# A delta rule with a low-rank mixer on one core: order estimated over all engines, two units' triangular blocks in 16x16, U^T x on four column groups

## Chip, core and metric

The kernel runs on one core of a Trainium2 chip. TensorE (PE; PEld is its loading of weights), VectorE (DVE), ScalarE (ACT), GpSimd (POOL) and SyncE (SP) each work through a queue of their own in order and wait for each other by semaphores. SP, ACT and POOL also issue transfers (SPq, ACTq, POOLq). The metric is device time in microseconds.

## What is computed

For 4 batches of 8 heads, 768 tokens and 48 channels: a delta rule with a state of 48x48 per head, and on its output, put together to 384 channels, a mixer with a matrix of rank 32 over tokens and two wide layers over channels. The inputs of the mixer (U, V, w_ch1, w_ch2) are float64; all else is float32.

```python
k_n = k / (norm(k) + 1e-6)
for t in range(768):
    y[t]  = q[t] @ state
    state = state + beta[t] * outer(k_n[t], v[t] - k_n[t] @ state)
x = y, heads side by side                 # (4, 768, 384)
u = x + ((x^T @ U) @ V)^T                 # rank 32 over tokens
out = u + relu(u @ w_ch1) @ w_ch2         # 384 -> 1536 -> 384
```

## The kernel before

**Units.** A batch is worked on in two units of 384 tokens (n = 0 to 7), a unit in six steps of 64 tokens, all heads together. `load` (line 256) fetches k, q, v of a unit by 24 transfers; `norms` (279) makes the norms of k and the factors cp; `grams` (325) transposes k and q on TensorE (p_t), copies them (kq) and multiplies k with k (pg) and k with q (qk). `blocks` (371) inverts a unitriangular 64x64 matrix per step and head: its two diagonal 32x32 blocks by substitution on VectorE, all 96 of a partition layout at once (gs is the blocks, fetched through HBM by scr; 31 steps of two instructions at lines 405 and 411, which write xt), then the block below by two rounds of 32x32 products on TensorE (p_x, p_v), for which xt goes through HBM (scr2) to zt and zc. `recur` (478) runs the steps: p_b (k times state), rhs, p_c (inverse times rhs), z, p_s (state's change), s, and two p_y.

**Mixer.** `front` (575) computes U^T x of a batch (p_tt, six matmuls into 32 partitions, then tt), adds V^T tt to x (p_h), and transposes x (p_u, ut); `wide` (616) runs the two wide layers on half a batch: p_f with relu (h_f), then p_o, a chunk being three matmuls (a float32 matmul is two instructions in the trace). `load_weights` (198) brings 27 slices of weights, whose float64 words VectorE and ScalarE turn into float32 by integer operations, five on VectorE a slice.

**Order.** Every part is a generator that yields what its next piece costs on TensorE and VectorE and a delay; `run` (96) takes, again and again, the piece that can start first by these numbers and lets it emit its instructions. What it emits first stands first in every engine's queue, SP's too; nothing is reordered later. PSUM has three pairs of buffers (pair, one, mix). In `load`, the next unit's loads start when the grams of the unit before are emitted and the recurrence two units back is done. Line 120 is the choice:

```python
start = max(ready[i], clock["pe"] if pe else 0, clock["dve"] if dve and not pe else 0)
```

Of the kernel before, what the change touches and what calls it, by code (L numbers as in the profile page):

```python
# [8 lines left out]
FP32 = mybir.dt.float32  # L9
# [6 lines left out]
L = 64  # L16
BK = 32
# [7 lines left out]
def kernel(  # L25
# [44 lines left out]
    step = ctx.enter_context(tc.tile_pool(name="step", bufs=3))  # L70
# [20 lines left out]
    done, clock = {}, {"now": 0.0, "pe": 0.0, "dve": 0.0}  # L91
# [4 lines left out]
    def run(parts):  # L96
        waits = {}
        ready = {}

        def advance(i, at):  # L100
            try:
                waits[i], ready[i] = next(parts[i]), at
            except StopIteration:
                waits.pop(i, None)

        for i in range(len(parts)):
            advance(i, 0.0)
        while waits:
            best = None
            for i in sorted(waits):  # L110
                step = waits[i]
                while i in waits and isinstance(waits[i][0], tuple):
                    keys = [k for k in waits[i] if k[1] >= 0]
                    if not all(k in done for k in keys):
                        break
                    advance(i, max([ready[i]] + [done[k] for k in keys]))
                if i not in waits or isinstance(waits[i][0], tuple):
# [3 lines left out]
                if best is None or start < best[0] - 1e-6:  # L121
                    best = start, i
            start, i = best
            pe, dve, after = waits[i]
            end = start + pe
            if pe:
                clock["pe"] = end
            if dve:
                end = clock["dve"] = max(end, clock["dve"]) + dve
            clock["now"] = end  # L130
            advance(i, end + after)
# [23 lines left out]

    bias_e = const.tile([128, 1], FP32, name="bias_e")
    nc.gpsimd.memset(bias_e, -896.0 * 2.0 ** 23)
    warm = const.tile([128, 1], FP32, name="warm")
    nc.scalar.sqrt(warm, ident[:, 0:1])
# [540 lines left out]
```

## Time and profile before

| what | us |
|---|---|
| median of 3 runs (lowest to highest) | 850.73 (849.42 to 859.04) |
| the profiled execution, whole | 850.8 |
| its span, first to last instruction | 849.1 |
| PE busy | 692.5 (82%) |
| PEld busy | 436.3 (51%) |
| DVE busy | 343.0 (40%) |
| ACT busy | 190.2 (22%) |
| POOL busy | 30.6 (4%) |
| mean granted TensorE clock, of full speed | 0.864 |

Busy shares are means over stages of different kinds. Matmuls are pipelined, so that the distance from the start of one to the start of the next says more than the duration of one. The chain that ended last is 55% PE, 17% DVE, 11% DMA and 8% SPq.

### The profile page before, as it was taken

What the parts mean: (1) busy time and instruction counts of PE and PEld (TensorE: products, weight loads), DVE (VectorE), ACT (ScalarE), POOL (GpSimd) and SP (SyncE); (2) the same over time, 40 slices, a digit from 0 to 9 for tenths busy, and PEclk for the clock granted to TensorE, in tenths of its full rate; (3) what the DMA queues carried; (4) which work ended last, traced back from release to release, by engine and by line L of the source; (5) the groups of instructions that cost most, each with busy time, mean ns of one, the idle gap of its engine ahead of it and who ended that gap; (6) DMA issues with size and microseconds to landing.
All of it is one profiled execution on the core that took longest, in us unless ns stands there. A gap on an engine that the chain in (4) does not pass through costs nothing.

```text
span 849.1 us, 17340 instructions
## 1 busy us (share of the span) xinstructions
PE 692.5 (82%) x7520; PEld 436.3 (51%) x7520; DVE 343.0 (40%) x884; ACT 190.2 (22%) x413; POOL 30.6 (4%) x59
## 2 busy tenths in 40 slices
PE   3430567758995899887989898998988999999998
PEld 2320565635553566563545565645555656455554
DVE  3659753474793831215728202166383101010000
ACT  2320213423320222232311133213320222021020
POOL 3100000020100000000000000000000000000000
PEclk9765555675997999986999999998989899999999
DMA  6722137172224020414040213041403000000000
GB/s 125 155 46 53 30 68 141 39 160 56 80 71 82 31 49 16 90 33 100 1 84 12 57 29 68 15 99 39 78 7 67 12 2 2 19 9 10 19 1 28
DMA packets 148083, 44.18 MB, mean 52 GB/s; under 512 B 141752, under 2 KB 144824, under 8 KB 148008
## 3 DMA queue, kind: packets, MB, share of 16 engines
q1 hardware_dynamic: 142720, 32.56, 19.2%
q0 software_dynamic: 2048, 9.83, 4.1%
q8 instruction: 59, 0.97, 0.5%
q10 hardware_dynamic: 3240, 0.69, 0.4%
q14 instruction: 16, 0.13, 0.1%
HBM read 31.95 MB, written 11.01 MB: 51 GB/s over the span
## 4 chain that ended last, share of the span: by engine, by line
PE 55%; DVE 17%; DMA 11%; SPq 8%; ACT 4%; issue 3%; POOL 1%; DVEq 0%; ACTq 0%; POOLq 0%
PE p_o L640 17%; PE p_f L623 17%; DVE xt L411 6%; DVE prod L405 5%; SPq L266 4%; PE p_c L524 3%; PE p_g L350 3%; DMA scr<-xt 3%; PE p_h L597 2%; PE p_y L554 2%; DMA gs<-scr 2%; PE p_t L338 2%; DMA scr<-pg 2%; PE p_s L538 2%; SPq L424 2%
## 5 line engine op out<-in xcount | busy, mean ns | idle before, releaser
L640 PE MATMUL p_o<-w_sb,h_f 128*128 128x384 f32 x576 | 209.2, 510 | 1.5 <-DVE w_sb L247 1.5
L623 PE MATMUL p_f<-ut,w_sb 128*128 128x384 f32 x576 | 208.1, 508 | 0.0
L640 PEld LDWEIGHTS p_o<-w_sb,h_f 128*128 128x128 f32 x576 | 108.1, 196 | 71.9 <-issue 11.9
L623 PEld LDWEIGHTS p_f<-ut,w_sb 128*128 128x128 f32 x576 | 108.0, 196 | 69.9 <-issue 8.7
L631 ACT ACTIVATE h_f<-p_f 128x384 f32<-128x384 f32 x96 | 47.1, 491 | 185.0 <-PE p_f L623 185.0
L411 DVE TENSOR_TENSOR xt<-xt,prod 96x31 f32<-96x31 f32 (+15 forms) x248 | 83.9, 338 | 8.7 <-DVE prod L405 0.3
L405 DVE TENSOR_TENSOR prod<-gs,xt 96x31 f32<-96x31 f32 (+15 forms) x248 | 83.4, 336 | 7.2
L647 DVE TENSOR_TENSOR x<-x,p_o 128x384 f32<-128x384 f32 x24 | 13.3, 553 | 131.8 <-PE p_o L640 131.8
L444 PE MATMUL p_x<-zt,pg 32*32 32x32 f32 x768 | 20.3, 216 | 49.9 <-DMA zt<-scr 49.7
L350 PE MATMUL p_g<-kq 48*64 48x128 f32 x768 | 36.1, 333 | 22.9 <-ACT kq L343 18.0
L547 DVE TENSOR_TENSOR s<-s,p_s 128x192 f32<-128x192 f32 x40 | 14.1, 352 | 91.8 <-PE p_s L538 91.5
L338 PE MATMUL p_t<-ident,qn 128*128 128x128 f32 x96 | 31.3, 341 | 23.9 <-DMA qn<-in_q_dram 18.8
L563 ACT COPY x<-p_y 64x192 f32<-64x192 f32 x96 | 30.1, 314 | 71.3 <-PE p_y L554 70.8
L444 PEld LDWEIGHTS p_x<-zt,pg 32*32 32x32 f32 x768 | 18.5, 131 | 53.4 <-issue 30.6
L350 PEld LDWEIGHTS p_g<-kq 48*64 48x64 f32 x768 | 27.1, 166 | 31.3 <-ACT kq L343 21.7
L508 DVE TENSOR_TENSOR rhs<-vn,p_b 128x192 f32<-128x192 f32 x44 | 15.4, 351 | 60.0 <-PE p_b L500 59.9
L524 PEld LDWEIGHTS p_c<-rhs,zt 64*64 64x64 f32 x704 | 29.0, 158 | 18.3 <-issue 11.3
L554 PE MATMUL p_y<-z,qk 64*64 64x48 f32 x768 | 37.0, 245 | 1.0 <-ACT z L532 1.0
L338 PE MATMUL p_t<-ident,kn 128*128 128x128 f32 x96 | 32.3, 352 | 6.2 <-DMA kn<-in_k_dram 4.2
L343 ACT COPY kq<-p_t 128x512 f32<-128x512 f32 x48 | 27.9, 584 | 37.0 <-PE p_t L338 34.7
L532 ACT COPY z<-p_c 128x192 f32<-128x192 f32 x48 | 15.3, 319 | 91.5 <-PE p_c L524 91.2
L524 PE MATMUL p_c<-rhs,zt 64*64 64x48 f32 x704 | 34.3, 245 | 1.8 <-DVE rhs L508 1.7
(71 smaller groups left out, 569.1 us busy)
## 6 DMA issues: line engine op xcount, KB each, us to landing
wide<-in_moe_w_ch_dram POOLq DMA_DIRECT2D x24, 384.0 KB, 3.7
vn<-in_v_dram SPq DMA_DIRECT2D x64, 72.0 KB
out_dram<-x SPq DMA_DIRECT2D x24, 192.0 KB
kn<-in_k_dram SPq DMA_DIRECT2D x60, 72.0 KB
qn<-in_q_dram SPq DMA_DIRECT2D x60, 72.0 KB
scr<-pg SPq DMA_DIRECT2D x32, 96.0 KB
gs<-scr SPq DMA_DIRECT2D x8, 384.0 KB
scr<-xt SPq DMA_DIRECT2D x8, 384.0 KB
```

The costliest lines, as they stand in the source:

```text
L266: queue.dma_start(out=t[L * g : L * g + L, :, s, 0:D], in_=src[b, 4 * g + s, hf * UC * L : (hf + 1) * UC * L, :].rearrange("(c t) d -> t c ...
L338: nc.tensor.transpose(p_t[:, j, i], t[:, c, 2 * j : 2 * j + 2].rearrange("p s d -> p (s d)"), ident,)
L350: nc.tensor.matmul(p_g[cols, par, c, :, j], kq[rows, c0 + c, j, 0, cols], kq[rows, c0 + c, j, :, cols], start=True, stop=True,)
L405: nc.vector.tensor_tensor(out=prod, in0=gs[:, j : j + 1, j + 1 :].to_broadcast([NP, m, w]), in1=xt[:, 0:m, j : j + 1].to_broadcast([NP, m, ...
L411: nc.vector.tensor_tensor(out=xt[:, 0:m, j + 1 :], in0=xt[:, 0:m, j + 1 :], in1=prod, op=ALU.subtract)
L444: nc.tensor.matmul(p_x[BK * g : BK * g + BK, r, BK * (e % (2 * UC)) : BK * (e % (2 * UC)) + BK], pg[rows, r, c, j, 0:BK], zt[rows, r, c, j ...
L524: nc.tensor.matmul(p_c[half(g), 2 * j + par], zt[half(g), par, cu, j], rhs[half(g), 2 * j + par], start=True, stop=True,)
L554: nc.tensor.matmul(p_y[half(g), par, D * j : D * j + D], qk[half(g), par, cu, j], z[half(g), 2 * j + par], start=(c == 0 and j == 0), stop ...
L563: nc.scalar.copy(x[half(c % 2), c // 2, 4 * D * g : 4 * D * (g + 1)].rearrange("p (j r d) -> p r j d", r=2, d=D), pair_of(p_y)[half(g)],)
L623: nc.tensor.matmul(p_f, w1_sb[:, t, f * 128 : (f + 1) * 128], ut[:, t], start=(t == 0), stop=(t == KT - 1),)
L631: nc.scalar.activation(h_f, p_f, ACTF.Relu)
L640: nc.tensor.matmul(p_o, hs[f][:, c * 128 - i * GT : (c + 1) * 128 - i * GT], w2_sb[:, f], start=(f == 0), stop=(f == FT - 1),)
```

## The change

It has three parts.

**The order.** A piece (`step`) now says what it costs on TensorE, VectorE, ScalarE and SP, which PSUM buffers it takes and which it gives back; `run` keeps a clock for each of the four and a list of free buffers. TensorE's costs count 1.6 times until the first `front`. Pieces are cut finer: a chunk's relu, a front's block of 128 tokens and an output row are parts of their own. Transposes go by k and q apart (two steps of k, or of q, in one p_t), and for units 0 and 1 the grams of k come ahead of those of q. Loads of k, q and v are pieces of four transfers each; q waits for the transposes of the unit before, k only for the recurrence two units back. The weights w_ch1 come by columns. beta and unit 0's v are issued on POOL. A slice of V is loaded four times, once for each 32 partitions.

**16x16.** For units 0 and 1 the substitution runs on the two 16x16 diagonal blocks of each 32x32 block (15 steps of two instructions, both blocks in one). Two rounds of products on TensorE, p_e and p_d, of 96 matmuls each with 32x32 weights and 16 columns, give the rest of the 32x32 block; p_d is written into zt by four ScalarE products and into zc by one VectorE instruction.

**U^T x.** Its six matmuls write four groups of 32 partitions (block c of tokens goes to group c % 4); V, standing four times, adds the groups up in p_h.

```diff
-                pe, dve, _ = waits[i]
-                start = max(ready[i], clock["pe"] if pe else 0, clock["dve"] if dve and not pe else 0)
+                engine = next((e for e in ("pe", "dve", "act", "sp") if s[e]), None)
+                at = max(
+                    [ready[i], clock[engine] if engine else 0.0]
+                    + [sorted(free[t])[s["take"].count(t) - 1] for t in s["take"]]
+                )
...
+            if s["pe"]:
+                ends["pe"] = clock["pe"] = at + s["pe"] * clock["slow"]
+            for e in ("dve", "act", "sp"):
+                if s[e]:
+                    ends[e] = clock[e] = max(clock[e], ends["pe"]) + s[e]
...
-        for t, src in ((kns[n % 2], k), (qn, q), (vn, v)):
+        for name, t, src in (("k", kns[n % 2], k), ("q", qn, q), ("v", vn, v)):
+            if name == "q":
+                yield need(("turned", n - 1))
             for g in range(2):
+                queue = nc.sync
+                if n == 0:
+                    queue = nc.gpsimd if name == "v" else (nc.sync, nc.scalar)[g]
+                yield step(sp=2.6 if queue is nc.sync else 0.0)
...
+        split = 2 if n < 2 else 1
+        SB = BK // split
...
-        for j in range(BK - 1):
-            m, w = j + 1, BK - 1 - j
+        for j in range(SB - 1):
+            m, w = j + 1, SB - 1 - j
...
+                for i in range(4):
+                    rows = slice(BK * i, BK * i + BK)
+                    nc.tensor.matmul(
+                        p_e[rows, e],
+                        pg[rows, r, c, j, BK * (i % 2) : BK * (i % 2) + BK],
+                        zc[rows, e, SB:BK],
...
+                    nc.tensor.matmul(
+                        p_d[rows, e], zn[rows, e], xe[rows, e], start=True, stop=True
+                    )
...
+                nc.scalar.mul(diagonal(zt, i)[0:SB, :, SB:BK], p_d[rows], -1.0)
...
-            p_t = ps_one([R, DM], "p_tt")
+            p_t = ps_one([128, DM], "p_tt")
             for c in range(NB):
...
-                    p_t, u_sb[:, c], x[:, c], start=(c == 0), stop=(c == NB - 1)
+                    p_t[R * (c % 4) : R * (c % 4) + R], u_sb[:, c], x[:, c],
+                    start=(c < 4), stop=(c + 4 >= NB),
```

Three places show how instructions moved. The first is SP's queue from the program's start; kn0 and kn1 are the keys of units 0 and 1, xt and pg of unit 0 come first. Before:

```order
L266 DMA kn0_92<-in_k_dram 64x6x48 x4
L266 DMA qn_94<-in_q_dram 64x6x48 x4
L266 DMA vn_117<-in_v_dram 64x6x48 x8
L316 DMA cp_247<-cts_245 24x32 x4
L266 DMA kn1_93<-in_k_dram 64x6x48 x8
L266 DMA qn_94<-in_q_dram 64x6x48 x8
L266 DMA vn_337<-in_v_dram 64x6x48 x8
L381 DMA scr_365<-pg_143 32x24x32 x4
L388 DMA gs_370<-scr_365 96x1024
```

And of the change:

```order
L309 DMA kn0_92<-in_k_dram 64x6x48 x4
L309 DMA qn_94<-in_q_dram 64x6x48 x4
L309 DMA kn1_93<-in_k_dram 64x6x48 x8
L360 DMA cp_291<-cts_264 24x32 x4
L455 DMA scr_365<-pg_120 32x24x32 x4
L360 DMA cp_408<-cts_381 24x32 x4
L464 DMA gs_450<-scr_365 96x1024
L455 DMA scr_545<-pg_125 32x24x32 x4
L309 DMA qn_94<-in_q_dram 64x6x48 x4
L464 DMA gs_577<-scr_545 96x1024
L309 DMA qn_94<-in_q_dram 64x6x48 x4
L509 DMA scr2_599<-xt_493 96x1024
```

Unit 1's q and v moved behind unit 0's scr and gs, its cp ahead of gs, and unit 0's v left the queue. The second place is TensorE's queue in the third and fourth step of the first recurrence, where the change has put unit 1's p_e (before, no other work stood there until p_x):

```order
L659 MATMUL p_b<-s,kq 64x48 x8
L667 MATMUL p_y<-s,kq 64x48 x8
L553 MATMUL p_e<-zc,pg 32x16 x24
L684 MATMUL p_c<-rhs,zt_95 64x48 x8
L553 MATMUL p_e<-zc,pg 32x16 x24
L699 MATMUL p_s<-z,kn_92 64x48 x8
L707 MATMUL p_y<-z,qk 64x48 x8
L553 MATMUL p_e<-zc,pg 32x16 x24
```

Each piece of 24 matmuls stands where TensorE's next step waits for rhs, z or s. The third place is TensorE's queue around the first U^T x. Before, with kn_93 and qn being unit 3's keys and queries:

```order
L554 MATMUL p_y<-z,qk 64x48 x8
L585 MATMUL p_tt<-x,u_sb 32x384 x6
L338 MATMUL p_t<-ident,kn_93 128x128
L338 MATMUL p_t<-ident,qn 128x128
L338 MATMUL p_t<-ident,kn_93 128x128
L338 MATMUL p_t<-ident,qn 128x128
L597 MATMUL p_h<-tt,v_sb 128x384
```

And of the change:

```order
L754 MATMUL p_tt<-x,u_sb 32x384 x6
L768 MATMUL p_h<-tt,v_sb 128x384 x2
L776 MATMUL p_u<-ident,x 128x128 x6
L768 MATMUL p_h<-tt,v_sb 128x384
L776 MATMUL p_u<-ident,x 128x128 x3
L768 MATMUL p_h<-tt,v_sb 128x384 x2
L809 MATMUL p_f<-ut,w_sb 128x384 x3
L776 MATMUL p_u<-ident,x 128x128 x6
L809 MATMUL p_f<-ut,w_sb 128x384 x3
L768 MATMUL p_h<-tt,v_sb 128x384
L385 MATMUL p_t<-ident,kn_93 128x128 x4
```

Unit 3's transposes moved behind the front and two chunks of p_f.

## Rows read from the trace of the kernel before

**Rows 1.** Timeline of TensorE (start us, us, engine, line, operation): the four U^T x.

```profile
178.19 5.91 PE L585 MATMUL p_tt<-x,u_sb 128*32 128x384 f32 x12
...
381.70 6.55 PE L585 MATMUL p_tt<-x,u_sb 128*32 128x384 f32 x12
...
562.32 4.06 PE L585 MATMUL p_tt<-x,u_sb 128*32 128x384 f32 x12
...
731.46 4.06 PE L585 MATMUL p_tt<-x,u_sb 128*32 128x384 f32 x12
```

**Rows 2.** Page, part 2: clock granted to TensorE, 40 slices, tenths of full speed.

```profile
PEclk9765555675997999986999999998989899999999
```

**Rows 3.** Timeline: ScalarE's last copy of unit 0's pg, and SP's queue.

```profile
25.53 5.40 SPq L266 DMA_DIRECT2D kn<-in_k_dram  x8
...
30.90 0.59 ACT L358 COPY pg<-p_g 128x512 f32<-128x512 f32 x1 [0.79 <-PE p_g L350]
...
41.83 2.40 SPq L381 DMA_DIRECT2D scr<-pg  x4
```

**Rows 4.** Timeline: unit 0's substitution on VectorE: first, a middle and last instruction.

```profile
49.61 1.22 DVE L392 TENSOR_TENSOR gs<-gs,cp 96x1024 f32<-96x1024 f32 x1 [10.54 <-DMA gs<-scr]
...
69.08 0.42 DVE L405 TENSOR_TENSOR prod<-gs,xt 96x256 f32<-96x256 f32 x1
...
80.86 0.21 DVE L411 TENSOR_TENSOR xt<-xt,prod 96x31 f32<-96x31 f32 x1
```

**Rows 5.** Timeline: unit 0's p_x and the first p_c.

```profile
89.86 2.77 PE L444 MATMUL p_x<-zt,pg 32*32 32x32 f32 x94 [1.66 <-DMA zt<-scr]
...
97.18 0.45 PE L524 MATMUL p_c<-vn,zt 64*64 64x48 f32 x2 [0.90 <-ACT zt L465]
```

**Rows 6.** Timeline of TensorE: the product that turns beta.

```profile
5.79 2.74 PE L175 MATMUL p_bt<-ident,beta_sb 16*64 16x16 f32 x46 [1.04 <-DMA beta_sb<-in_beta_dram]
```

**Rows 7.** Timeline of TensorE: p_b of two recurrence steps that follow each other.

```profile
105.95 0.68 PE L500 MATMUL p_b<-s,kq 48*64 48x48 f32 x16 [0.74 <-ACT x L563]
...
110.87 0.68 PE L500 MATMUL p_b<-s,kq 48*64 48x48 f32 x16 [0.74 <-ACT x L563]
```

**Rows 8.** Page, part 6 (KB each, us to landing), and VectorE's groups until 260 us.

```profile
wide<-in_moe_w_ch_dram POOLq DMA_DIRECT2D x24, 384.0 KB, 3.7
...
L243 DVE SCALAR_TENSOR_TENSOR power<-wide,power 128x384 int32<-128x384 int32 (+2 forms) x27 | 14.6, 542 | 5.8 <-ACT power L230 5.8
```

**Rows 9.** Timeline of TensorE: p_x between other work.

```profile
312.80 1.70 PE L444 MATMUL p_x<-zt,pg 32*32 32x32 f32 x94 [0.44 <-DMA zt<-scr]
314.43 0.67 PE L524 MATMUL p_c<-rhs,zt 64*64 64x48 f32 x16
```

**Rows 10.** Timeline of TensorE: a step of the second batch's recurrence, with chunks.

```profile
294.31 0.45 PE L500 MATMUL p_b<-s,kq 48*64 48x48 f32 x16 [1.06 <-DVE s L551]
...
294.92 2.20 PE L623 MATMUL p_f<-ut,w_sb 128*128 128x384 f32 x6
...
297.05 0.67 PE L524 MATMUL p_c<-rhs,zt 64*64 64x48 f32 x16
...
302.75 0.45 PE L500 MATMUL p_b<-s,kq 48*64 48x48 f32 x16
```

**Rows 11.** Timeline and chain: a p_h, and 12 chunks behind each other.

```profile
737.58 0.91 PE L597 MATMUL p_h<-tt,v_sb 32*128 32x384 f32 x2
...
822.10 23.23 PE p_o L640 x72
```

**Rows 12.** Timeline of TensorE: four transposes, the chunk behind them, and one gram.

```profile
418.82 0.27 PE L338 MATMUL p_t<-ident,kn 128*128 128x128 f32 x1
...
419.26 1.13 PE L623 MATMUL p_f<-ut,w_sb 128*128 128x384 f32 x3
...
423.67 1.10 PE L350 MATMUL p_g<-kq 48*64 48x128 f32 x32
```

**Rows 13.** Timeline of TensorE behind the first U^T x.

```profile
193.03 0.48 PE L338 MATMUL p_t<-ident,qn 128*128 128x128 f32 x1 [6.84 <-DMA qn<-in_q_dram]
```

More of the change, by code (lines that the diff above doesn't have):

```diff
@@ L88, in ps_mix, with need, step, advance @@
         return psum.tile(shape, FP32, name=name, tag="mix", bufs=2)
-    done, clock = {}, {"now": 0.0, "pe": 0.0, "dve": 0.0}
+    done = {}
+    clock = dict(now=0.0, pe=0.0, dve=0.0, act=0.0, sp=0.0, slow=1.6)
+    free = dict(pair=[0.0] * 2, one=[0.0] * 2, mix=[0.0] * 2)
+    def need(*keys):
+        return [k for k in keys if k[1] >= 0]
+    def step(pe=0.0, dve=0.0, act=0.0, sp=0.0, then=0.0, on=None, take=(), give=()):
+        return dict(pe=pe, dve=dve, act=act, sp=sp, then=then, on=on, take=take, give=give)
     def emitted(key, after=0.0):
         done[key] = clock["now"] + after
[L96 to L107, printed above, removed]
+    parts, waits, ready = {}, {}, {}
+    def advance(i, at):
+        try:
+            waits[i], ready[i] = next(parts[i]), at
+        except StopIteration:
+            del waits[i]
+    def begin(part, place):
+        i = (place, len(parts))
+        parts[i], waits[i] = part, []
+        advance(i, clock["now"])
+    def run():
         while waits:
@@ L120, in run @@
-                start = max(ready[i], clock["pe"] if pe else 0, clock["dve"] if dve and not pe else 0)
[L121 to L131, printed above, removed]
+                while isinstance(waits.get(i), list) and all(k in done for k in waits[i]):
+                    advance(i, max([ready[i]] + [done[k] for k in waits[i]]))
@@ new lines, in run @@
+                if best is None or at < best[0] - 1e-6:
+                    best = at, i
+            at, i = best
+            s = waits[i]
+            for t in s["take"]:
+                free[t].remove(min(free[t]))
+            ends = {"pe": at}
+            if s["pe"]:
[3 more added lines that the diff above has]
+                    ends[e] = clock[e] = max(clock[e], ends["pe"]) + s[e]
+            clock["now"] = max(ends.values())
@@ L134 @@
+            for t in s["give"]:
+                free[t].append(clock["now"] + 0.1)
+            advance(i, ends.get(s["on"], clock["now"]) + s["then"])
     ident = const.tile([128, 128], FP32, name="ident")
@@ L181, in beta_thread @@
                 )
+        yield step(dve=0.4, give=("one",))
         nc.vector.tensor_copy(out=betas, in_=p_bt)
@@ L250, in load_weights @@
             )
[L251 removed]
+            emitted(("weights", i), 0.2)
     raw, made, xs, states = {}, {}, {}, {}
@@ L308, in norms @@
         )
-        yield 0.3, 1.3, 0.5
+        yield step(pe=0.2, then=0.15, take=("one",))
         p_ct = ps_one([CS, 128], "p_ct")
@@ L440, in blocks @@
+        yield step(dve=1.0, then=-0.8)
+        zn = turned(zc)
+        place = [slice(64 * split // 2 * g, 64 * split // 2 * g + BK) for g in range(2)]
         for e in range(CS):
+            if e % 8 == 0:
+                yield step(pe=0.57, take=("pair",) if e == 0 else ())
+            if e == 0:
+                p_x = ps_pair("p_x")
             r, c, j = e // (2 * UC), e // 2 % UC, e % 2
@@ L519, in recur @@
                     )
-            yield 0.6, 0, 0.9
+                yield step(dve=0.37, then=0.1, give=("pair",))
+                rhs = steps.tile([128, 4, D], FP32, name="rhs", bufs=2)
+                nc.vector.tensor_tensor(
+                    out=by_slot(rhs), in0=by_slot(vn), in1=pair_of(p_b), op=ALU.subtract
+                )
+            yield step(pe=0.4, then=0.1, take=("one",))
             p_c = ps_one([128, 4, D], "p_c")
```

435 lines of the change are left out of this document (270 added, 165 removed).

## The prediction, on record before the changed kernel was run

> **What bounds the kernel now.** I read the page's 40 slices first, then the order of time of TensorE, SP and VectorE. The four places where U^T x of a batch starts on TensorE [rows 1] cut the span of 849.1 us into five pieces: 178.2 until the first, then 203.5, 180.6 and 169.2 from one to the next, and 117.6 from the last to the end. In the first piece nothing of the wide layers can run, since the first batch's recurrence must end first; the clock granted to TensorE there is half, 1.2 of 2.4 GHz, for most of it [rows 2]. It is a chain of small steps: loads, grams, scr and gs through HBM, VectorE's substitution, the joining of the 32x32 blocks, twelve recurrence steps. In the three middle pieces one batch's wide layers (48 chunks of three matmuls) run between the next batch's recurrence steps: TensorE's work is the bound there as long as its queue is not stuck at a wait. The last piece is the last batch's wide layers alone.
>
> **The sum's form.** New time = A (to the first U^T x) + 3 C (one batch to the next) + D (last U^T x to the end) + 1.7, the part of the profiled execution's 850.8 that lies outside its span. The median shown, 850.73, is the same, so the result stands against it too.
>
> **A, the first piece (178.2 now).** Unit 0's pg is complete at 31.5, but SP issues unit 1's 24 loads first, from 25.53 on, so that scr<-pg stands at 41.83, and VectorE, waiting for gs, begins at 49.61 [rows 3, 4]. In the new SP order scr comes ahead of unit 1's q and v. Two things hold it: the four cp transfers of unit 1, now between scr and gs (about 3.2), and ScalarE, whose four q issues stand behind the first weight conversion; I take pg at 32.5, scr issued by 35, cp to 38.6, gs landed and VectorE free at 42.5: 7 earlier.
>
> The substitution of unit 0 takes until scr2 at 81.1 now, 31.5, with unit 1's norms in it. New: 15 steps of two instructions on two small blocks of 30 to 128 elements. A row of 31 elements takes 0.21, one of 256 takes 0.42 [rows 4]; on that line the mean is 0.27, 0.30 from start to start: 9.0, with half a gs product and one qk 10. End: 52.5. What was moved with it: scr2, then four v loads of unit 1 (2.8 of SP), then four zc; I take zc landed at 61, 8.5 behind, as p_x now begins 8.8 behind the substitution [rows 4, 5].
>
> Added: the join. p_e and p_d are 192 instructions each of 32x32 weights and 16 columns. The nearest row is p_x, 94 in 2.77 at half clock, 29.5 ns each [rows 5]; the other end is p_bt, 16 columns with other weights, 46 in 2.74, 60 ns [rows 6]. I take p_x, whose weights have the same shape: 5.7 each; the other end adds 5.8 to each. With unit 1's transposes and grams between the pieces of p_e (2.6), its copy (0.7) and the four ScalarE products from p_d (2.0), the first half of the join is over at 78. From p_x to p_c takes 7.3 now [rows 5]; a second xz copy and ScalarE's conversions in front make it 9.4: the recurrence starts at 87.4 instead of 97.2. So unit 0 gains only 9.8, although its substitution is 21 shorter.
>
> The recurrence: a step at half clock takes 4.92 [rows 7], twelve take 59; today the stretch takes 81, since unit 1's zt, unit 2's loads and grams are waited for in order. New: 59, plus p_e and p_d of unit 1 in eight pieces between the steps (11.4, of which I let 9 count, since TensorE waits little in a step), p_x and p_v 5.5, unit 2's transposes and grams 8, and 3 for the weights: two slices a step now stand ahead of rhs and s on VectorE. A slice lands in 3.7 and takes VectorE five instructions of about half a microsecond (one is the 0.542 of the row) [rows 8]; with two buffers that is one per about 3.1, 6.2 a step for six steps, partly beside p_e. That is 84.5: **A = 172**, 6 less than now.
>
> Weighed here: p_x (32x32 weights) and the p_c behind it (64x64) start 1.63 apart, which is what 94 instructions of 17 ns take; no gap for the change of shape is to be seen [rows 9]. The Trainium skill ("TensorEngine Tiling (Array Packing)", Tiling Modes, Key Properties) says that a change of tiling mode drains TensorE, which speaks against pieces of p_e and p_d between 64x64 work. Were each of the sixteen changes to cost 0.4, the sum would be 6 higher; by the row it is nothing.
>
> **C, batch to batch (203.5, 180.6, 169.2 now).** TensorE's work in one: a recurrence step with three chunks takes 8.44, a chunk in it 2.13, so the step itself 2.05 [rows 10]; a chunk behind another chunk takes 23.23 / 12 = 1.94 [rows 11]. In the new order 43 of 48 chunks stand alone: 101.3. Steps 24.6; twelve groups of four transposes at 0.44 and six grams at 1.1: 11.9 [rows 12]; p_x and p_v four times 1.63: 6.5 [rows 9]; six p_h at 0.9, 5.4 [rows 11]; p_u 2.0; U^T x. U^T x takes 4.0 now [rows 1]. On four column groups: nothing before shows this form. The ends are 4.0, if the groups run one after the other, and 1.2: grams in four tiles pass 128 columns in 1.1/32 = 0.034 a piece where whole-array transposes take 0.11 [rows 12], 3.2 times as many. I take 1.7. The sum is 153.4; with today's U^T x 155.7.
>
> Today's order leaves three chunks behind the third U^T x and five behind the fourth. With that made even the three pieces are 203.5, 187 and 173.4, so 48, 31 and 18 are lost to waits and to the half clock behind them. Part of it is unit 3's transposes, queued directly behind U^T x with loads that SP has not yet issued: TensorE stands 6.84 at one of them [rows 13]. In the new order p_h, p_u and the first p_f come first; by the prices above unit 3's k is needed 16 behind U^T x and has landed 10 behind, p_x of unit 2 is reached 53 behind and its zt has landed 49 behind, p_x of unit 3 at 95 against 91. Also, all weight conversions are over by then; today they lie between unit 2's substitution steps. What is left to lose: the end of the recurrence and the front are uncovered now (U^T x waits for the last x, tt, x and ut one for another, 4 to 5), and behind such waits part of the front runs at half clock (4), and 2 elsewhere: 10.6. **C = 164.**
>
> **D (117.6 now).** Without the five chunks left over, 107. U^T x saves 2.3, the front loses its cover, 8 as above: **D = 113**.
>
> Sum: 172 + 492 + 113 + 1.7 = **779**.
>
> **Rivals.**
> First, the clock: the denser first piece lifts TensorE's clock before the first U^T x. For it: pieces of p_e and p_d fill waits; against: today's busy recurrence stays at half [rows 2]. The steps would fall from 4.92 to what VectorE's weights allow, and A to about 154: 761. Chance 0.15.
> Second, the join is dearer than p_x: at p_bt's 60 ns [rows 6] it adds 11 on unit 0's chain and about 8 between the steps, A = 191: 798. The zc path through HBM, shared with v loads, would show in the same place. Chance 0.20.
> Third, the estimated order does not keep TensorE fed: each C loses the 18 of today's best piece, C = 171.4: 801. For it: the queues are in order and the estimates are numbers; against: the distances of 4 and more found above. Chance 0.13.
> Fourth, U^T x does not run side by side; that part of the change then does nothing: 2.3 in each of four, 788. Chance alone 0.04.
> Fifth, not faster at all: the weights. All 27 slices now stand on VectorE ahead of the first batch's last steps; if the other loads, moved beside them, delay the slices, each late slice stops rhs and s. 71 over 24 slices are 3.0 each; with two buffers a slice must then land in 9.7 instead of 3.7 for the time to reach 850. For it: all loads of units 0 and 1 share the first 60 us; against: the median of 3.7 holds today beside the same loads [rows 8]. Chance 0.04.
> The forecast itself: 0.44.
>
> **How the numbers follow.** 779 is the likeliest case. Below it lies the first rival at 761, above it the others at 788 to 801; A's own error is some 10 and C's 3 for each of three, so I give 752 to 813, which leaves out the fifth rival and the tails of the first and third. A change within 1% is about what a measurement of this kernel can't tell from none: only cases between the fifth rival and the others would land there, 0.02; slower by over 1%, 0.04; faster, 0.94.
>
> **What would show it.** U^T x starting near 172, 336, 500 and 664; gs on VectorE near 42.5; substitution of unit 0 over near 52.5; p_c of unit 0 near 87; p_e and p_d near 5.7 each for 192; U^T x under 2 when its x is there; between two U^T x no wait over 2 at p_x or at transposes. I am wrong if A stays at 178 or more, if C stays above 172, or if VectorE waits for weight slices during the recurrence.

## Result, and the profile after

The changed kernel takes 731.71 us (median of 4 runs, 726.95 to 737.04) against 851.93 of the kernel before beside it: a ratio of 0.858, 95% interval 0.850 to 0.866. The forecast was 779 with a range of 752 to 813: right in its sign, wrong in its size. The profiled execution took 726.95, with a span of 725.1, and is the fastest of the four.

The rows that answer to [rows 1] and [rows 2] are the four U^T x, in TensorE's timeline (start us, us, engine, line, operation), and the page's clock row:

```profile
162.04 1.83 PE L754 MATMUL p_tt<-x,u_sb 128*32 128x384 f32 x12
...
314.64 1.83 PE L754 MATMUL p_tt<-x,u_sb 128*32 128x384 f32 x12
...
467.33 1.83 PE L754 MATMUL p_tt<-x,u_sb 128*32 128x384 f32 x12
...
616.61 2.59 PE L754 MATMUL p_tt<-x,u_sb 128*32 128x384 f32 x12
```

```profile
PEclk9975555599999999999999999999999999999999
```

The view by windows shows the five pieces that these starts cut: first of the changed kernel, then of the kernel before (busy us of each engine with its instructions, then TensorE's granted clock, DMA share, GB/s).

```profile
core 0: us, PE busy (x) PEld busy (x) DVE busy (x) ACT busy (x) POOL busy (x), PEclk, DMA share, GB/s
0.00:162.04 162.04, 99.31 (x2667) 85.37 (x2667) 102.27 (x260) 59.36 (x118) 33.51 (x70) 0.68 0.57 125
162.04:314.64 152.60, 150.52 (x1873) 94.10 (x1869) 70.54 (x187) 43.59 (x97) 3.64 (x4) 1.00 0.27 56
314.64:467.33 152.69, 150.51 (x1873) 94.10 (x1869) 70.63 (x187) 43.58 (x97) 3.60 (x4) 1.00 0.27 56
467.33:616.61 149.28, 145.66 (x1752) 89.62 (x1748) 65.24 (x177) 37.15 (x85) 1.21 (x2) 1.00 0.22 45
616.61:725.10 108.49, 102.66 (x332) 59.24 (x330) 7.21 (x13) 14.97 (x32) 0.00 (x0) 0.99 0.03 11
```

```profile
178.19:381.70 203.51, 172.15 (x1870) 106.12 (x1868) 99.44 (x252) 50.38 (x109) 10.29 (x17) 0.89 0.28 64
381.70:562.32 180.62, 162.50 (x1853) 98.48 (x1851) 71.73 (x191) 43.94 (x98) 2.37 (x4) 0.92 0.23 49
562.32:731.46 169.14, 156.70 (x1743) 94.09 (x1742) 62.72 (x170) 37.10 (x84) 1.18 (x2) 0.94 0.16 34
731.46:849.10 117.64, 113.05 (x355) 63.59 (x354) 8.30 (x15) 14.33 (x30) 0.00 (x0) 0.99 0.04 14
```

Of the 107.8 that the last four pieces lost (670.9 to 563.1), 52.8 are idle time of TensorE (66.5 to 13.7 over the four) and 55.0 are busy time. U^T x itself is 12.5 of the busy time (20.6 to 8.1 over the four); the rest goes along with the granted clock, at which nearly the same instructions pass: its mean in the four pieces was 0.89, 0.92, 0.94 and 0.99 and is 1.00, 1.00, 1.00 and 0.99. In a middle piece TensorE is now busy for 150.5 of 152.6.

The first piece, by the timeline (for [rows 4] and [rows 5]): VectorE's first and last instruction of unit 0's substitution, a piece of 48 of p_e, most of p_d, the first p_c.

```profile
40.90 0.68 DVE L478 TENSOR_TENSOR gs<-gs,cp 96x512 f32<-96x512 f32 x1
...
50.57 0.21 DVE L501 TENSOR_TENSOR xt<-xt,prod 96x30 f32<-96x30 f32 x1
```

```profile
64.20 0.84 PE L553 MATMUL p_e<-zc,pg 32*32 32x16 f32 x48
...
67.88 1.90 PE L570 MATMUL p_d<-xe,zn 32*32 32x16 f32 x128 [0.97 <-issue]
...
84.74 0.44 PE L684 MATMUL p_c<-vn,zt 64*64 64x48 f32 x2 [1.97 <-ACT zt L623]
```

### The profile page after: what moved, and what is told of

Read it like the earlier page. It is cut to its first block, busy times and chain, and to the rows that moved or that the text cites. A ratio compares the mean times of both kernels' runs of the same rounds, so it can differ in the third digit from the quotient of the medians.

```text
span 725.1 us, 19244 instructions
## 1 busy us (share of the span) xinstructions
PE 648.7 (89%) x8480; PEld 422.4 (58%) x8480; DVE 315.9 (44%) x824; ACT 198.6 (27%) x426; POOL 42.0 (6%) x80
## 4 chain that ended last, share of the span: by engine, by line
PE 80%; DMA 6%; DVE 3%; issue 3%; SPq 3%; ACT 2%; POOL 2%; ACTq 0%; DVEq 0%; POOLq 0%
PE p_o L825 27%; PE p_f L809 26%; PE p_c L684 4%; PE p_y L707 3%; PE p_g L400 3%; PE p_t L385 3%; PE p_s L699 2%; DMA wide<-in_moe_w_ch_dram 2%; PE p_b L659 2%; SPq L309 2%; PE p_v L616 2%; PE p_x L595 2%; DMA gs<-scr 2%; PE p_y L667 2%; PE p_h L768 1%
## 5 line engine op out<-in xcount | busy, mean ns | idle before, releaser
L809 PE MATMUL p_f<-ut,w_sb 128*128 128x384 f32 x576 | 203.4, 494 | 0.6 <-ACT ut L779 0.6
L825 PE MATMUL p_o<-w_sb,h_f 128*128 128x384 f32 x576 | 201.2, 495 | 0.0
L809 PEld LDWEIGHTS p_f<-ut,w_sb 128*128 128x128 f32 x576 | 103.6, 190 | 61.5 <-issue 1.5
L501 DVE TENSOR_TENSOR xt<-xt,prod 96x112 f32<-96x112 f32 (+21 forms) x216 | 70.5, 326 | 7.7 <-DVE prod L495 0.3
L495 DVE TENSOR_TENSOR prod<-gs,xt 96x112 f32<-96x112 f32 (+21 forms) x216 | 70.1, 324 | 6.5
L400 PE MATMUL p_g<-kq 48*64 48x128 f32 (+1 forms) x960 | 32.5, 285 | 11.1 <-ACT kq L391 11.1
L707 PEld LDWEIGHTS p_y<-z,qk 64*64 64x64 f32 x768 | 30.5, 152 | 0.6 <-ACT z L693 0.6
L699 PEld LDWEIGHTS p_s<-z,kn 64*64 64x64 f32 x704 | 16.1, 149 | 25.2 <-issue 16.1
L385 PE MATMUL p_t<-ident,qn 128*128 128x128 f32 x96 | 18.1, 317 | 12.6 <-DMA qn<-in_q_dram 12.6
L419 DVE TENSOR_TENSOR qk<-p_g,mask_u 128x256 f32<-128x256 f32 x48 | 18.0, 416 | 23.8 <-ACT pg L413 23.8
```

Source lines behind the costliest of these rows:

```text
L385: nc.tensor.transpose(p_t[:, x, j], t[:, c, 2 * j : 2 * j + 2].rearrange("p s d -> p (s d)"), ident,)
L400: nc.tensor.matmul(p_g[cols, par, c, parts, j], kq[rows, c0 + c, j, 0, cols], kq[rows, c0 + c, j, parts, cols], start=True, stop=True,)
L495: nc.vector.tensor_tensor(out=prod, in0=gb[:, :, j : j + 1, j + 1 :].to_broadcast([NP, split, m, w]), in1=xb[:, :, 0:m, j : j + 1].to_broa ...
L501: nc.vector.tensor_tensor(out=xb[:, :, 0:m, j + 1 :], in0=xb[:, :, 0:m, j + 1 :], in1=prod, op=ALU.subtract,)
L699: nc.tensor.matmul(p_s[half(par), g, D * j : D * j + D], kn[half(g), cu, 2 * j + par], z[half(g), 2 * j + par], start=True, stop=True,)
L707: nc.tensor.matmul(p_y[half(g), par, D * j : D * j + D], qk[half(g), par, cu, j], z[half(g), 2 * j + par], start=(c == 0 and j == 0), stop ...
```

## Experiments

All runs in one table: time (ratio to the kernel before beside it, with interval), and the five pieces of the profiled execution.

| kernel | us | ratio (95%) | to first U^T x | 2nd | 3rd | 4th | last |
|---|---|---|---|---|---|---|---|
| before | 850.73 | | 178.2 | 203.5 | 180.6 | 169.1 | 117.6 |
| changed | 731.7 | 0.858 (0.850-0.866) | 162.0 | 152.6 | 152.7 | 149.3 | 108.5 |
| e_one_group | 760.6 | 0.892 (0.886-0.898) | 165.9 | 159.2 | 157.8 | 155.5 | 114.5 |
| e_whole32 | 750.2 | 0.881 (0.876-0.886) | 160.6 | 176.7 | 156.3 | 148.9 | 107.3 |
| e_order_only | 784.1 | 0.920 (0.911-0.928) | 160.3 | 180.9 | 168.8 | 156.4 | 114.3 |
| e_old_order | 846.8 | 0.993 (0.989-0.997) | 190.0 | 191.6 | 179.8 | 168.7 | 109.0 |
| e_one_group_wide_h | 739.5 | 0.866 (0.860-0.872) | 169.6 | 154.2 | 154.1 | 151.2 | 111.7 |
| e_narrow_h | 750.5 | 0.879 (0.875-0.884) | 170.1 | 157.6 | 156.9 | 152.9 | 110.9 |
| e_keep_clock | 737.7 | 0.865 (0.861-0.870) | 173.3 | 151.8 | 153.6 | 148.7 | 107.5 |
| e_join_by_tile | 745.5 | one run | 181.7 | 152.5 | 153.1 | 148.7 | 107.5 |
| e_four_tiles | 728.2 | 0.845 (0.839-0.852) | 172.1 | 150.0 | 150.6 | 148.0 | 107.3 |
| e_late_tt | 764.6 | 0.892 (0.885-0.899) | 170.2 | 160.9 | 160.6 | 156.5 | 116.4 |
| e_full_speed | 732.6 | 0.855 (0.848-0.861) | 156.2 | 165.1 | 151.8 | 149.1 | 107.5 |
| e_no_act_clock | 729.0 | 0.850 (0.844-0.857) | 156.2 | 160.0 | 153.6 | 149.9 | 107.6 |
| b_long_trip | 844.8 | 0.987 (0.979-0.994) | 171.3 | 204.4 | 179.7 | 172.2 | 117.6 |
| e_short_trip | 769.4 | 0.899 (0.893-0.904) | 171.8 | 166.8 | 161.5 | 161.6 | 107.4 |
| b_wide_h | 840.9 | 0.982 (0.974-0.990) | 183.0 | 200.4 | 180.0 | 162.4 | 115.6 |

The first piece differs between executions of the same program part: the changed kernel, e_one_group and e_narrow_h have the same order up to the first U^T x, which stands at 162.0, 165.9 and 170.1. Their first p_c is at 84.7 to 86.2; what differs with it is when the granted clock rises from 0.5 to 1.0: at 147.8, at 156.3, and in e_narrow_h only at 172.1, behind the first U^T x. Why it rises earlier in one execution than in another is not shown. So runs are compared here by the pieces behind it; one profiled execution stands for each run.

### The parts apart

e_one_group (U^T x on one group, p_h on 32 rows):

```diff
-                    p_t[R * (c % 4) : R * (c % 4) + R], u_sb[:, c], x[:, c],
-                    start=(c < 4), stop=(c + 4 >= NB),
+                    p_t[0:R], u_sb[:, c], x[:, c],
+                    start=(c == 0), stop=(c + 1 == NB),
...
-                p_h, v_sb[:, c * 128 : (c + 1) * 128], tt, start=True, stop=True
+                p_h, v_sb[0:R, c * 128 : (c + 1) * 128], tt[0:R], start=True, stop=True
```

> The changed kernel with U^T x on one column group again (12 instructions of 128x384 into 32 partitions, p_h then reads 32 rows); every queue keeps its order. If TensorE's queue is the bound there, each U^T x grows from 1.83 to about 4.06 and the span from 725.1 to about 734, each piece by 2.2. Rival, U^T x was hidden behind the last copies of x: the span stays within 725 to 728.

e_whole32:

```diff
-        split = 2 if n < 2 else 1
+        split = 1
```

> The changed kernel with all units by 32x32 substitution, without p_e and p_d; order by the same planner. Theory, the order makes the time and the small blocks little: unit 0's substitution then ends near 63 instead of 50.6, but p_x follows 9 behind and p_c 7 behind that, near 80 against 84.7 with the join; U^T x near 157 to 165, span 720 to 730. Rival, the short substitution is worth what it takes off VectorE (10 to 20 in the first piece): U^T x at 172 or later, span 735 or more.

e_order_only has both edits.

> The changed kernel's order alone: 32x32 substitution for all units and U^T x on one column group. Order theory: the sum of the two runs beside it, span 729 to 739; of the 124 that the span lost, some 115 come from the order. Rival, substitution and U^T x carry a good part: 745 or more.

e_old_order is the kernel before with the new `blocks` for units 0 and 1 (p_e and p_d in one piece each), the new U^T x and V in four copies, under the old `run`; of its edit the pieces that the old planner sees:

```diff
+        yield 3.2, 1.0, 0.7
+        zn = turned(zc)
+        p_e = ps_one([128, CS, SB], "p_e")
...
+        yield 3.2, 0.6, 2.0
+        p_d = ps_one([128, CS, SB], "p_d")
...
-                yield 0.65, 0, 0.0
+                yield 0.27, 0, 0.0
```

> The kernel before, with its own planner, its loads and its transposes, and only the 16x16 substitution with p_e and p_d (each in one piece) for units 0 and 1 and U^T x on 4 column groups. Order theory: the three middle pieces stay near 200, 178 and 166 (203.5, 180.6, 169.2 before, less 2 to 4 for U^T x), the granted clock in them at 0.9; the first U^T x at 165 to 178; span 825 to 842. Rival, the shorter substitution frees VectorE and TensorE's queue: middle pieces below 165, span below 800.

In the sum of the last four pieces: before 670.9; the new order alone 620.4; with the blocks too (e_one_group) 587.0; with U^T x too (e_whole32) 589.1; with both 563.1. The old order with both is at 649.1. The third and fourth piece of e_old_order stay at 179.8 and 168.7, as the order theory said; its first is 190.0, 12 above the upper end of what was expected, of which the later first p_c (101.8 for 97.2) is 4.6 and the rest is open. Its second is 191.6 instead of 203.5, but the second U^T x starts at 381.6 as before (381.7): what the second piece gains, the first has lost. So of the 21.8 that its last four pieces are shorter, only 10.0 are a gain of the whole span. So the order is the largest part, but each of the others is worth over 31 on top of it, far beyond what I had expected of them, and together only those 10.0 without it. Two questions came of it.

What the blocks are worth lies not where they are. The first piece is 160.6 without them, as short as with them: the first p_c stands at 85.6 (84.7 with them). But VectorE does 118.6 of work in the first piece instead of 102.3, and unit 2's norms no longer fit there: its cp is issued at 172.9 instead of 143.8. Its substitution begins 38 later (first row: changed kernel, second: e_whole32):

```profile
171.39 1.22 DVE L478 TENSOR_TENSOR gs<-gs,cp 96x1024 f32<-96x1024 f32 x1 [2.69 <-DMA gs<-scr]
```

```profile
209.53 1.22 DVE L478 TENSOR_TENSOR gs<-gs,cp 96x1024 f32<-96x1024 f32 x1 [8.67 <-DMA gs<-scr]
```

The second batch's steps then begin so late that the first batch's chunks have run out at 300, and seven steps run alone, at a clock of 0.56 (by windows, e_whole32):

```profile
300.00:337.00 37.00, 31.64 (x664) 27.50 (x662) 8.18 (x19) 11.98 (x30) 1.39 (x1) 0.56 0.35 67
```

### U^T x, or p_h?

e_one_group cost 23.9 in the four pieces, of which U^T x's own 4.06 for 1.83 (5.33 for 2.59 in the last) explains 9.4. Two runs part U^T x from p_h. e_one_group_wide_h keeps one group for U^T x, copies it into rows 0 to 31 of a tt whose other rows are zero, and lets p_h read 128 rows:

```diff
-            tts[b] = mix.tile([128, DM], FP32, name="tt", bufs=1)
-            nc.vector.tensor_copy(out=tts[b], in_=p_t)
+            tts[b] = tt_all
+            nc.vector.tensor_copy(out=tts[b][0:R], in_=p_t[0:R])
```

> The changed kernel with U^T x on one column group, but p_h reads 128 rows as in the changed kernel (rows 32 to 127 of tt are zero). The run with one group and a p_h of 32 rows cost 28 in the span, 9 of them U^T x itself; behind each U^T x the granted clock went to 0.5 for some 8. Theory, the narrow U^T x alone brings the clock down: the same here, span 748 to 756, clock near 0.90. Rival, the 32 rows of p_h do it: span near 734, clock near 0.92 as in the changed kernel.

e_narrow_h has the last pair of e_one_group's diff alone (p_h on 32 rows), which leaves out three of the four partial sums of U^T x.

> The changed kernel with U^T x on 4 column groups, but p_h reads 32 rows only, which leaves out three of the four partial sums of U^T x. Theory, U^T x brings the clock down and not p_h: span 723 to 729, no fall of the granted clock behind U^T x. Rival, p_h of 32 rows: 740 or more, with a stretch at 0.5 behind each U^T x.

My theory fell: with the narrow U^T x alone the four pieces are 1.6, 1.4, 1.9 and 3.2 longer, about U^T x's own time, and the clock in the middle ones is 0.99 to 1.00. With the p_h of 32 rows alone they are 5.0, 4.2, 3.7 and 2.4 longer although U^T x takes 1.83, and the granted clock falls to half for 7 to 10 each time, 2 to 3 behind the start of the first p_h. The windows of e_narrow_h behind the U^T x of 327.67, then of the changed kernel behind that of 314.64:

```profile
329.50:333.50 4.00, 3.25 (x12) 1.79 (x12) 1.67 (x3) 0.82 (x2) 0.00 (x0) 0.88 0.80 128
333.50:337.50 4.00, 3.26 (x7) 1.38 (x7) 0.62 (x2) 0.62 (x2) 0.00 (x0) 0.50 0.85 190
337.50:341.50 4.00, 4.00 (x7) 1.83 (x6) 3.75 (x10) 1.16 (x1) 0.00 (x0) 0.50 0.60 109
```

```profile
316.50:320.50 4.00, 3.28 (x12) 1.60 (x12) 1.67 (x3) 0.96 (x2) 0.00 (x0) 1.00 0.82 133
320.50:324.50 4.00, 3.26 (x12) 1.83 (x12) 0.97 (x2) 0.48 (x1) 0.00 (x0) 1.00 0.80 180
```

At the same distance from U^T x TensorE is as busy in both (3.25 and 3.28, then 3.26 and 3.26 of 4.00), so here it is not the waits. The four copies of V, which I had not costed at all, are the larger half of that part of the change (15.2 of its 23.9 in the four pieces, the columns of U^T x 8.1).

b_wide_h makes the same change of V and tt in the kernel before.

> The kernel before with V in four copies over the partitions and p_h reading 128 rows of tt (rows 32 to 127 zero); U^T x on one column group and the order as before. Theory, the clock no longer falls behind U^T x for p_h's sake: the last piece 3 to 5 shorter (117.6 before), the three middle pieces together 4 to 12 shorter, since in them the clock also falls behind waits; span 832 to 842. Rival, in the old order other waits bring the clock down all the same: the last piece within 1.5 of 117.6 and the span within 4 of 849.

The last four pieces are 3.1, 0.6, 6.7 and 2.0 shorter, 10.4 in the middle ones (4 to 12 expected) and 2.0 in the last (3 to 5 expected). Of these 12.4 the first piece loses 4.8 again, for which I have no cause beyond the spread above. The reason that the theory gave does not hold for the last piece: in the kernel before the clock did not fall in that front at all, although its six p_h read 32 rows. They stood between other products, as these rows show (the kernel before, then b_wide_h), and the window of the kernel before has the clock:

```profile
735.44 2.20 PE L640 MATMUL p_o<-w_sb,h_f 128*128 128x384 f32 x6
737.58 0.91 PE L597 MATMUL p_h<-tt,v_sb 32*128 32x384 f32 x2
738.41 2.20 PE L640 MATMUL p_o<-w_sb,h_f 128*128 128x384 f32 x6
```

```profile
731.80 0.81 PE L602 MATMUL p_h<-tt_all,v_sb 128*128 128x384 f32 x2
732.44 2.10 PE L645 MATMUL p_o<-w_sb,h_f 128*128 128x384 f32 x6
```

```profile
731.46:760.00 28.54, 27.73 (x89) 13.53 (x89) 4.67 (x9) 4.14 (x9) 0.00 (x0) 1.00 0.04 14
```

A p_h is followed by the next product after 0.83 there and after 0.64 here; six times that is 1.1 of the 2.0. In the first front of the kernel before the clock fell ahead of the first p_h, within the wait of 6.84 of [rows 13] (two windows, and that p_h):

```profile
182.50:188.50 6.00, 1.90 (x6) 0.47 (x4) 5.34 (x15) 1.05 (x2) 1.74 (x3) 1.00 0.82 175
189.00:193.00 4.00, 0.00 (x0) 0.00 (x0) 0.34 (x1) 0.00 (x0) 0.00 (x0) 0.50 0.86 191
194.00 1.64 PE L597 MATMUL p_h<-tt,v_sb 32*128 32x384 f32 x2
```

And e_old_order, whose p_h reads 128 rows, has in the 30 us behind its four U^T x a mean clock of 0.64, 0.70, 0.89 and 1.00, where the kernel before has 0.61, 0.69, 0.89 and 1.00, and b_wide_h 0.71, 0.83, 1.00 and 1.00. So in the old order waits bring the clock down by themselves, and what p_h's rows add there stays open; in the new order, with the long waits gone, the rows decide.

### What a wait costs, and the estimates behind the order

e_late_tt makes tt late:

```diff
-            nc.vector.tensor_copy(out=tts[b], in_=p_t)
+            for _ in range(13):
+                nc.vector.tensor_copy(out=tts[b], in_=p_t)
```

> The changed kernel with the copy of tt made 13 times instead of once, so that TensorE waits some 6.7 more behind each U^T x. Theory, a wait of this length costs itself and no more: each of the last four pieces 6 to 7 longer, the granted clock in them stays at 1.0. Rival, the clock falls behind such a wait as it does behind the p_h of 32 rows: each 10 to 11 longer, with a stretch at 0.5.

The changed kernel's wait for tt, then this run's (us in all, times, longest):

```profile
PE p_h L768 <- DVE tt L760: 2.6, 4, 0.7
```

```profile
PE p_h L769 <- DVE tt L761: 31.4, 4, 7.9
```

The waits grew by 7.2 each and the four pieces by 8.3, 7.9, 7.2 and 8.0: a wait costs itself and up to 1 more. The theory was right about the price and the rival about the clock, which falls to half within the wait (windows behind the second U^T x; the first p_h starts at 340.8):

```profile
333.00:338.00 5.00, 0.00 (x0) 0.00 (x0) 4.72 (x9) 0.00 (x0) 0.00 (x0) 1.00 0.77 127
338.50:340.80 2.30, 0.02 (x1) 0.06 (x1) 2.02 (x4) 0.00 (x0) 0.00 (x0) 0.50 0.85 222
```

It stays there for 7 to 10 in each of the four, part of it while TensorE waits anyway.

b_long_trip and e_short_trip change estimates alone:

```diff
-        yield 0, 0, 6.0
+        yield 0, 0, 9.0
```

```diff
-        yield step(sp=2.3, then=2.2)
+        yield step(sp=2.3)
-        yield step(sp=0.4, then=3.2)
+        yield step(sp=0.4)
```

(each at scr, gs and scr2, zt).

> The kernel before with its planner's two estimates of the trip through HBM (scr to gs, and scr2 to zt) at 9.0 instead of 6.0; all work the same, only the order moves. Theory, the short estimate makes the waits of 2 to 7 at p_x and the falls of the clock behind them: in the window from 178 to 849 TensorE's waits for zt go from 18.3 to below 6, the third and fourth pieces from 180.6 and 169.1 to 172 or less and 160 or less, span 815 to 835. Rival, the order lacks more than this number (no clocks of SP and ScalarE, no banks, transposes in one part): waits move elsewhere, span 840 or more.

> The changed kernel with the waiting times of its planner's trips through HBM (scr to gs 2.2 and 3.2, scr2 to zt 2.2 and 2.2) at 0; all work the same. Theory, as with the kernel before and its 6.0: p_x stands too early in TensorE's queue, waits of 2 to 6 at p_x, the clock falls behind some, the three middle pieces 4 to 10 longer each. Rival, other work stands close enough behind: within 2 of 152.6, 152.7, 149.3.

In the old kernel the waits for zt fell as expected (behind the first U^T x: before, then b_long_trip), but others grew, and the middle pieces are no shorter:

```profile
PE p_x L444 <- DMA zt<-scr: 18.3, 11, 7.3
```

```profile
PE p_x L444 <- DMA zt<-scr: 6.2, 3, 3.9
PE p_u L605 <- DVE x L600: 7.7, 7, 2.7
PE p_v L459 <- ACT xz L452: 6.4, 3, 2.9
```

In the changed kernel the short estimates cost 14.2, 8.8 and 12.3 (4 to 10 expected), but not at p_x, where the theory had put waits of 2 to 6. Between its first and its last U^T x TensorE's longest waits by sum are for x, and p_x has only short ones:

```profile
PE p_u L776 <- DVE x L772: 7.2, 4, 5.0
PE p_x L595 <- DMA zt<-scr: 5.5, 5, 1.6
```

The clock's mean in the three pieces is 0.95 to 0.97. So this estimate has to be near the truth, though its error was paid in other places than the theory had put it, and correcting one number of the old planner is not enough. Which of its other lacks holds its third piece at 180 was not parted further.

e_full_speed (first) and e_no_act_clock (second):

```diff
-    clock = dict(now=0.0, pe=0.0, dve=0.0, act=0.0, sp=0.0, slow=1.6)
+    clock = dict(now=0.0, pe=0.0, dve=0.0, act=0.0, sp=0.0, slow=1.0)
```

```diff
-            for e in ("dve", "act", "sp"):
+            for e in ("dve", "sp"):
```

> The changed kernel with the planner's TensorE at full clock from the start (factor 1.0 instead of 1.6 until the first U^T x); all work the same, only the order moves. Theory, the order is tolerant of such an error: the last four pieces within 3 of the changed kernel's (152.6, 152.7, 149.3, 108.5). Rival, the estimate of the half clock is what places unit 2's norms and grams ahead of the first U^T x: unit 2's substitution begins 20 or more later than 171.4 and the second piece is 165 or more, as in the run with 32x32 blocks.

> The changed kernel with ScalarE left out of the planner's clocks (its queue taken as free); all work the same. Theory, it is the banks, the finer pieces and unit 2's head start that keep TensorE fed, not ScalarE's clock: last four pieces within 5 of the changed kernel's in all. Rival, ScalarE's estimate matters: TensorE waits for ScalarE's copies (kq, pg, z), 4 or more in each piece.

The factor does place unit 2, as the rival said: its substitution begins at 194.7 (180.5 without ScalarE's clock) instead of 171.4, and the second piece is 165.1. But U^T x then comes 5.8 earlier: first and second piece together are 321.3 and 316.2 against 314.6. The first piece alone can make such a difference, though that it does so here is not shown. The others stay within 1. So the bounds of both theories were missed (12.5 longer in the second piece of e_full_speed instead of 3; 8.0 in all in e_no_act_clock instead of 5), and still neither number carries the gain: by the whole time the two runs are at 732.6 and 729.0 against 731.7. The head start itself shows in a row of four: unit 2's substitution begins 9, 24, 38 and 49 behind the first U^T x (changed kernel, e_no_act_clock, e_full_speed, e_whole32), and the second piece is 152.6, 160.0, 165.1 and 176.7.

### Tiles, and the clock of the first piece

e_join_by_tile turns the loops of p_e and p_d round (p_d alone shown):

```diff
-                for i in range(4):
+                for i in range(4) if e % 6 == 5 else ():
                     rows = slice(BK * i, BK * i + BK)
-                    nc.tensor.matmul(
-                        p_d[rows, e], zn[rows, e], xe[rows, e], start=True, stop=True
-                    )
+                    for f in range(e - 5, e + 1):
+                        nc.tensor.matmul(
+                            p_d[rows, f], zn[rows, f], xe[rows, f], start=True, stop=True
+                        )
```

> The changed kernel with p_e and p_d ordered by tile within each piece of 24: six products of one 32x32 tile in a row, then six of the next, where the change goes round the four tiles; all other work the same. Theory, 17 a piece at half clock (48 instructions in 0.83) is four tiles running beside each other: by tile a piece takes 1.4 or more, p_e and p_d of two units together some 9 more, U^T x at 164 to 171. Rival, an instruction takes what its 16 columns take (p_x with 32 columns takes 29 ns): 0.83 as before, U^T x at 162.

A piece, in the timeline, against 0.84 above:

```profile
68.19 2.18 PE L554 MATMUL p_e<-zc,pg 32*32 32x16 f32 x48
```

45 ns an instruction instead of 17, same weights, same columns, both at half clock. The theory holds. Sixteen pieces at 1.34 more are 21, and the first piece of this one run is 19.7 longer, where I had expected U^T x at 171 at most. The Trainium skill ("TensorEngine Tiling (Array Packing)", Tiling Modes, Key Properties) states that different tiles work in parallel; these rows agree.

e_four_tiles uses it for p_x and p_v of units 2 to 7:

```diff
-                    p_x[place[g], r, BK * (e % (2 * UC)) : BK * (e % (2 * UC)) + BK],
+                    p_x[to, r, at : at + BK],   # to: 32 partitions for each (g, j)
...
-                    p_v[L * g : L * g + BK, r, at], zn[place[g], e], xz[place[g], r, at],
+                    p_v[L * g : L * g + BK, bank, at], z_of, x_of,   # bank = j
```

> The changed kernel with p_x and p_v of units 2 to 7 on four 32x32 tiles instead of two: the odd pairs of a chunk get partitions of their own in zc, p_x and xz, and p_v of odd pairs goes to the second bank. By the run with the join ordered by tile, tiles run beside each other: p_x and p_v of a unit from 1.7 each to about 0.9, two units in a piece, so 3 less in each of three pieces, span 9 to 12 less than the changed kernel's with the same first piece. Rival, two tiles that share their rows or columns don't run beside each other: pieces unchanged within 1.

A p_x of it, and of the changed kernel, both at full clock:

```profile
222.45 1.02 PE L600 MATMUL p_x<-zt,pg 32*32 32x32 f32 x96
225.53 1.02 PE L629 MATMUL p_v<-xz,zn 32*32 32x32 f32 x96
```

```profile
212.45 1.71 PE L595 MATMUL p_x<-zt,pg 32*32 32x32 f32 x96
216.22 1.71 PE L616 MATMUL p_v<-xz,zn 32*32 32x32 f32 x96
```

Four products of a piece save 0.69 each, 2.8 in all, a little less than the 3 expected; the middle pieces are 2.6, 2.1 and 1.3 shorter. Its 728.2 lies 3.5 below the changed kernel's time, less than the runs of either differ among themselves (722.7 to 735.2, and 727.0 to 737.0): its gain is read from the pieces, not from the time.

e_keep_clock puts products of the identity, which nothing reads, into TensorE's waits of the first piece (at p_c; the other places likewise):

```diff
             p_c = ps_one([128, 4, D], "p_c")
+            keep(3 if b == 0 else 0)
...
+    def keep(count):
+        p_k = ps_mix([128, 512], "p_k") if count else None
+        for i in range(count):
+            nc.tensor.matmul(
+                p_k[:, 128 * (i % 4) : 128 * (i % 4) + 128], ident, ident,
+                start=True, stop=True,
+            )
```

> The changed kernel with products of the identity by itself, into a bank that nothing reads, in TensorE's queue of the first piece: 36 ahead of unit 1's first q transposes (where it waits 12.3), 6 ahead of p_x and of p_v of unit 0, 3 ahead of p_c and 3 ahead of p_s in each of the twelve steps. Theory, the half clock holds the steps of the first piece (4.9 to 6.3 each; 3.0 each for the last two steps of the last batch, at full clock): the granted clock rises well before 148, U^T x starts at 138 to 152, span 700 to 715. Rival, the clock does not rise and the added products stand in the way (84 of 0.28 are 23, about 12 of it in waits): U^T x at 168 to 178, span 733 or more.

The rival was right: until 146.7 the clock rose only for spells of 7 to 10 and fell again, and the added products stood in the way: U^T x starts at 173.3 (two windows, and the page's row):

```profile
95.00:100.00 5.00, 4.71 (x174) 4.09 (x175) 3.71 (x9) 1.68 (x5) 0.54 (x1) 0.95 0.31 88
115.00:120.00 5.00, 5.00 (x105) 4.61 (x97) 2.73 (x6) 1.46 (x4) 1.07 (x2) 0.50 0.56 146
```

```profile
PEclk9985675599999999999999999999999999999999
```

At 115 to 120 TensorE was busy all the time, 3.0 of the 5.0 with the added 128x128 products, and stayed at half.

## Why the prediction was wrong

The sum was A 172 + 3 C of 164 + D 113 + 1.7. The profiled execution has 162.0 + 152.6 + 152.7 + 149.3 + 108.5 + 1.85: 10.0 less in A, 37.4 in the three C, 4.5 in D.

**C: the step that failed.** The work's sum, 153.4, was near: TensorE is busy for 150.5. Wrong was what I added for losses, 10.6, where the piece has 2.1 of idle time and no half clock. Its first term, the wait for the last x, tt, x and ut (4 to 5), measured 1.8 to 2.1 of idle time in the 30 us behind U^T x, the longest wait 0.74. Its second, the front at half clock (4), is not there: the clock stays at 1.00. The 2 elsewhere are not there either.

The half clock was carried over from the kernel before without its cause. In its first front it fell within a wait of 6.84 for unit 3's queries (q), and the new order, by the prediction's own account, puts unit 3's transposes behind the front. With waits of 0.65 and 0.74 nothing of that is left; e_late_tt, with waits of 7.8, has the fall again. A second cause I had not seen: had p_h still read 32 rows, the clock would have fallen all the same, and a piece would have been 2.4 to 5.0 longer (e_narrow_h), about the 4 that I had put down to waits: with such a p_h the size would have come out right by luck. The four copies of V, made for U^T x, took it away.

**D.** Its 8 for a front without cover was the same error, and a miscount hid part of it. The kernel before leaves four chunks behind the fourth U^T x, not five (168 instructions of p_o stand behind it, where a batch has 144, six to a chunk). Without them its last piece is 109.1, with the shorter U^T x 106.8; 108.5 is 1.7 more, not 8. By the same count the kernel before lost 16 in its best piece, not 18.

**The range.** With nothing lost in C and D the sum is 172 + 460 + 107 + 1.7 = 741. I had the sum of the work and did not use it as the lower end; 752 stood in its place. Even 741 lies above the measured 731.7, by less than the 10 that I had given as A's error.

**A.** gs at 40.9 (42.5 said), substitution over at 50.8 (52.5), zc in use from 58.1 to 60.0 (61), the first half of the join over at 74.7 (78), p_c at 84.7 (87.4): the chain was right. p_e and p_d were mis-sized: 17 ns an instruction, not p_x's 29.5 [rows 5] or p_bt's 60 [rows 6]. I chose by the weights' shape, but what counts is how many tiles follow one another: p_x goes round two, p_e four. The recurrence took 77.3 here and 83.9 in e_narrow_h, against 84.5; so part of the 10 is the luck of one execution, the fastest of the four. Of the 9.8 that unit 0 gains, the sum gave 7 to the earlier gs and 2.8 to the blocks with their join; e_whole32 has the first p_c only 0.9 later, so nearly all of it is the order's (scr at 31.0 instead of 41.8).

**What the blocks and U^T x are worth.** The sum gave the blocks next to nothing in A, which was right, and nothing behind, which was not; they are worth 26 behind, by unit 2's head start. I gave U^T x 2.3 in each of four; its columns are worth 1.4 to 3.2 and p_h's rows 2.4 to 5.0 more.

**The weighed rule.** No drain of 0.4 shows here either:

```profile
96.33 0.83 PE L553 MATMUL p_e<-zc,pg 32*32 32x16 f32 x48
97.09 1.09 PE L684 MATMUL p_c<-rhs,zt 64*64 64x48 f32 x16
```

The p_c (64x64) starts 0.76 behind the p_e (32x32), and 48 instructions of p_e take 0.70 by themselves (96 of them, at 61.75, are followed after 1.41).

**Rivals and signs.** The clock did not rise in the first piece before 148, and added products lifted it in spells only. The join was cheaper, not dearer. The third rival had the sign reversed: the estimated order keeps TensorE fed. Of my three signs of being wrong two stayed away, although the forecast was wrong; they looked only for a slower kernel. The third came by the letter: VectorE waited for weight slices seven times in the recurrence, 8.8 in all and at most 2.4 at a time, and the weights were over at 134 even so.

## To carry to other kernels

Where a queue-bound piece will be reordered, the lower end of the range is the sum of its work at full clock; each loss carried over from the old trace needs a cause, read from its rows, that still stands in the new program. A shortened chain may pay nothing where it is and much where the freed engine lets the next stage start sooner: look for what the planner can pull ahead. Small products are priced by the number of tiles that follow one another, so let the loop over tiles be the inner one.

## Seen of the hardware, not expected

- In the new order p_h with 32 rows of weights is followed by a granted clock of half for 7 to 10, from 2 to 3 behind the first of six; with 128 rows (the other 96 meeting partial sums, or zeros), the same count, columns and waits, it stays full. Between products of the wide layers (the last front of the kernel before) it stayed full with 32 rows too.
- Within waits of 6.84 (the kernel before) and 7.8 (e_late_tt) the clock falls to half; behind waits of 0.65 and 0.74 it stays full.
- 32x32 products of 16 columns take 17 ns going round four tiles and 45 ns six in a row on one, at half clock; 32x32 ones of 32 columns at full clock take 17.8 (1.71 for 96) on two tiles and 10.6 on four.
- A TensorE that is busy without a gap for 5 us, 3.0 of them with 128x128 products of the identity and the rest with 32x32 and 64x64 ones, can stay at half clock (115 to 120 in e_keep_clock).
- The same order of instructions reaches the same point at 162 or at 170; the later one goes with a later rise of the clock (147.8 and 172.1).
